# Top-k attention and a gated feed-forward layer on one core: eight units turned by TensorE in place of four, the steps as a list, the threshold kept negated

## The chip, the cores and the metric

One core of a Trainium2 chip runs the whole program. The metric is the device time of one execution in microseconds; the median of the runs is compared. A profile of one further execution shows every instruction of the five engines: TensorE (PE, its weight loads PEld), VectorE (DVE), ScalarE (ACT), GpSimd (POOL) and SyncE (SP), which here only issues transfers.

## What is computed

```
q, k, v: 8 batches x 8 heads x 576 rows x 64, float32
scores = q k^T / 8                                (576 x 576 per head)
kth    = the 32nd largest score of each row
attn   = softmax of the scores that are >= kth, the others masked away
x      = (attn v), heads side by side             (4608 tokens x 512)
h      = x w_in                                   (512 x 2048)
out    = (h * cos h) w_out                        (2048 x 512)
```

The weights come as 64-bit floats and are decoded to 32 bits on the chip.

## The kernel before

**Units and slots.** The 4608 tokens are cut into 36 blocks of 128. A block has four units, one for each pair of heads, so there are 144 units; a unit's scores are 128 rows x 2 heads x 576. The main loop has one slot for each unit. In slot i VectorE searches unit i for its 32 largest scores a row; ScalarE masks and exponentiates unit i-1 and copies the scores of unit i+1 out of PSUM (`take_scores`, L250); unit i-2 is turned, so that keys lie on partitions; TensorE makes the scores of units i+1 or i+1 and i+2, once in four slots the value matmuls of a whole block (`values`, L465 and after), and in between the feed-forward work of earlier blocks.

**The search.** Scores are folded: `rest` holds the larger of columns k and k+288 (L267), `low` the smaller (GpSimd: a sum, L283, less `rest`, L292; in slots 8 to 10, BUSY, VectorE itself, L275). Four rounds of eight largest on `rest` and two on `low` (L359, L364) leave two sorted lists. `merge_first` and `merge_second` (L347, L352) make the threshold from them. `bounds` (L372) writes the negated maximum and threshold, `distances` (L379) their difference nd. ScalarE scales nd (L386), masks with a Prelu whose bias is the negated threshold (L388) and takes exponentials with their sums (L396). `sums` and `reciprocal` (L404, L409) make 1/sum, named rden, at the end of the search in the next slot.

**Turning a unit.** There are two ways. `turn` (L430 and after), for units 0 to 3: eight 128x128 transposes on TensorE into two PSUM banks (L438), one more for the rest of the keys (L441) and two matmuls that spread rden (L445); ScalarE copies each bank into `ring` (L439, L446). `send`, for all others: GpSimd splits the numbers into 16-bit halves (L419, L421), SP writes them to DRAM (L450) and reads them back through a transposing transfer into `ring` (L456).

**Feed-forward.** `ff1` (L562) multiplies a block by w_in, 32 matmuls to a PSUM bank; ScalarE empties it twice (`take_first`, L576 and L578), GpSimd reduces (L598, L607), ScalarE takes the sine (L617, with a table load, and another before the next exponentials), GpSimd gates (L624), `ff2` (L637) multiplies by w_out, ScalarE scales (L647) and sends the result. The PSUM tag "mm" has two banks in turn: the transposes' `tt`, the banks of `ff1` and of `ff2` all come from it.

**Weights.** 32 chunks are loaded (L120) into staging tiles, 16 of w_in and 16 of w_out; ScalarE decodes each in two operations (`decode_first`, L133 and L136), VectorE shifts (`decode_second`, L151, two chunks in one instruction where they are neighbours) and GpSimd adds (`decode_third`, L160). This goes on until slot 11.

**What sets the order.** Every engine works through its own instructions in program order and waits by semaphores. The program order of a slot is written in `slot` (L762); which feed-forward pieces go where comes from `plan` (L755), from counters in `ff` and from conditions such as `can_first` (L654). `drain` (L832) ends the program.

Of the kernel before, what the change touches and what calls it, by code (L numbers as in the profile page):

```python
# [17 lines left out]
P = 128  # L18
# [12 lines left out]
def kernel(  # L31
# [63 lines left out]
    BUSY = range(8, 11)  # L95
    ff = {"live": 0, "tick": 0, "now": 0, "end": False, "kind": 0, "half": 0, "open": 0, "late": False}

    wq = {"next": 0, "loaded": deque(), "second": deque(), "third": deque(), "done": 0, "ready": 0}

    def staged(spare=0):  # L100
        return sum(c[2] == spare for k in ("loaded", "second", "third") for c in wq[k])

    def load_weights(n, queue):
        for _ in range(n):
            i = wq["next"]
            if i >= len(chunks):
                return
            src, dst = chunks[i]
            if not DECODE:
                queue.dma_start(out=dst[0][:, dst[1]], in_=src)  # L110
                wq["next"] = wq["done"] = i + 1
                continue
            spare = i < 2 * NC + 10 and i % 2 == 1 and staged(1) < XB
            if spare:
                st = ffw.tile([P, CW, 2], I32, tag="x", name="st", bufs=XB)
            elif staged() + ff["live"] >= CHUNKS:
                return
            else:
                st = ffw.tile([P, CW, 2], I32, tag="g", name="st", bufs=CHUNKS)
            queue.dma_start(out=st.rearrange("p w i -> p (w i)"), in_=src)  # L120
            wq["loaded"].append((st, dst, int(spare)))
            wq["next"] = i + 1

# [3 lines left out]
    def decode_first(n):  # L127


        for _ in range(min(n, len(wq["loaded"]))):  # L130
            st, w, spare = wq["loaded"].popleft()
            lo, hi = st[:, :, 0], st[:, :, 1]
            nc.scalar.activation(  # L133
                out=w[0][:, w[1]], in_=hi.bitcast(F32), func=AF.Prelu, scale=2.0**-111, alpha=2.0**32
            )
            nc.scalar.mul(out=lo, in_=lo.bitcast(U32), mul=2.0**-29)  # L136
            wq["second"].append((st, w, spare))

    def decode_second(n):

        left = min(n, len(wq["second"]))
        while left:
            st, (w, c), spare = wq["second"].popleft()
            wq["third"].append((st, (w, c), spare))
            m = 1
            if left > 1 and wq["second"][0][1][0] is w:
                wq["third"].append(wq["second"].popleft())
                m = 2
            left -= m
            wi = w[:, c : c + m].bitcast(I32)  # L150
            nc.vector.tensor_scalar(  # L151
                out=wi, in0=wi, scalar1=3, scalar2=None, op0=ALU.logical_shift_left
            )

    def decode_third():

        while wq["third"]:
            st, w, _ = wq["third"].pop()
            wi = w[0][:, w[1]].bitcast(I32)
            nc.gpsimd.tensor_tensor(out=wi, in0=wi, in1=st[:, :, 0], op=ALU.add)  # L160
            wq["done"] += 1

# [69 lines left out]
    def scores(u):  # L235
        sc = u["sc"] = ps.tile([P, 2, 512], F32, tag="sc", name="sc", bufs=2)
        for to, k0, k1 in ((sc, 0, SB), (sc_ends[u["n"] % 2], SB, S)):
            for b, q0, rows, r0 in u["parts"]:
                for j in range(2):
                    d = slice(j * D, (j + 1) * D)  # L240
                    st = pairs[b, u["hp"]]
                    nc.tensor.matmul(  # L242
                        to[r0 : r0 + rows, rim_bank(r0, j) if k0 else place(u["hp"], j), 0 : k1 - k0],
                        st["q"][d, q0 : q0 + rows],
                        st["k"][d, k0:k1],
                        start=True,
                        stop=True,
                    )
# [61 lines left out]
    def topk_first(u, w):  # L310

        u["top"] = tops[u["n"] % len(tops)]
        if w:
            merge_first(w)
        if u["n"] not in BUSY:
            fold_sum(u)
        fold_high(u)
        if w:
            merge_second(w)
        if u["n"] in BUSY:  # L320
            fold_now(u)
        topk_round(u, 0, [lambda: bounds(w), lambda: distances(w)] if w else ())

    def topk_round(u, rnd, between=(), ahead=None):
        top, rest, lasts = u["top"], u["rest"], TOPK // 8 - 1
        end = TOPK - 1 - 8 * rnd
        at = top[:, :, end : end - 8 if rnd < lasts else None : -1, 0]
        search(
            at, rest[:, :, HS:S] if rnd == 0 else rest[:, :, 0:HS], rest[:, :, 0:HS], rnd < lasts,
            between if rnd < lasts else (),  # L330
        )
        if rnd < lasts:
            return
        del u["rest"]
        low = u.pop("low")
        for k in range(TOPK // 16):
            more = k < TOPK // 16 - 1
            if ahead and not more:
                ahead()
            search(top[:, :, 1 + 8 * k : 9 + 8 * k, 1], low, low, more, () if more else between)  # L340

# [7 lines left out]
    def merge_second(u):  # L351
        nc.vector.tensor_reduce(  # L352
            out=u["top"][:, :, TOPK - 1, 1], in_=u.pop("lesser"), axis=mybir.AxisListType.X,
            op=ALU.max,
        )

    def search(to, src, rest, more, between=()):
        for j in range(2):
            nc.vector.max(to[:, j], src[:, j])  # L359
            if between:  # L360
                between[j]()
        if more:
            for j in range(2):
                nc.vector.match_replace(rest[:, j], to[:, j], src[:, j], NEG)  # L364

    def bounds(u):

        top = u.pop("top").rearrange("p j r i -> p j (r i)")
        end = 2 * TOPK
        less = u["less"] = top[:, :, end : end + 2]  # L370
        u["near"] = top[:, :, end - 1 : end + 1]
        nc.vector.tensor_reduce(  # L372
            out=less, in_=top[:, :, end - 2 : end].unsqueeze(3), axis=mybir.AxisListType.X,
            op=ALU.max, negate=True,
        )

    def distances(u):
        u["nd"] = small.tile([P, 2], F32, tag="nd", name="nd")
        nc.vector.tensor_reduce(  # L379
            out=u["nd"], in_=u.pop("near"), axis=mybir.AxisListType.X, op=ALU.add  # L380
        )

    def mask(u):

        s, less = u["s"], u.pop("less")
        nc.scalar.mul(out=u["nd"], in_=u["nd"], mul=SCALE)  # L386
        for j in range(2):
            nc.scalar.activation(  # L388
                out=s[:, j], in_=s[:, j], func=AF.Prelu, bias=less[:, j, 1:2], scale=1.0, alpha=FAR
            )  # L390

    def exponentials(u):
        s, nd = u["s"], u.pop("nd")
        den = u["den"] = dens[u["n"] % len(dens)]
# [16 lines left out]
    def both(u):  # L411
        return [lambda: sums(u), lambda: reciprocal(u)] if u else ()

    def split(u):


        s = u.pop("s").rearrange("p j k -> p (j k)").bitcast(U16)
        halves = work.tile([P, 2, 2 * S + P], U16, tag="halves", name="halves", bufs=1)
        nc.gpsimd.tensor_copy(out=halves[:, :, 0 : 2 * S], in_=s.rearrange("p (k h) -> p h k", h=2))  # L419
        rden = u.pop("rden").bitcast(U16).rearrange("p (j h) -> p h j", h=2)  # L420
        nc.gpsimd.tensor_copy(  # L421
            out=halves[:, :, 2 * S :].rearrange("p h (j d) -> p h j d", j=2),
            in_=rden.unsqueeze(3).to_broadcast([P, 2, 2, D]),
        )
        u["halves"] = halves
# [4 lines left out]
    def turn(u):  # L430

        s = u.pop("s").rearrange("p j k -> p (j k)")
        pT = u["pT"] = ring[:, u["n"] % RING]
        for half in range(2):
            tt = ps.tile([P, 512], F32, tag="mm", name="tt", bufs=2)
            for c in range(NT):
                at = (half * NT + c) * P
                nc.tensor.transpose(tt[:, c * P : (c + 1) * P], s[:, at : at + P], ident)  # L438
            nc.scalar.copy(out=pT[:, half * NT : (half + 1) * NT], in_=tt.rearrange("p (c q) -> p c q", c=NT))  # L439
        at = 2 * NT * P  # L440
        nc.tensor.transpose(room[0][:, P : 2 * P], s[:, at : at + P], ident)  # L441
        rden = u.pop("rden")
# [3 lines left out]
        nc.scalar.copy(out=pT[:, 2 * NT :], in_=rim[:, :, 3 * P :])  # L446
# [43 lines left out]
    def take_values(us):  # L490
# [4 lines left out]
        while i < n:  # L495
            at, h = us[i]["n"] % RING, (hp + i) // 2
            m = 4 if n - i == 4 and at + 4 <= RING else 2 if at + 2 <= RING else 1
            if m > 1:
# [7 lines left out]
            else:  # L506
                for k in range(i, i + 2):
# [3 lines left out]
                    )  # L511
                m = 2
            i += m
        blk["left"] -= n
        blk["tick"] = ff["tick"]


# [393 lines left out]
```

## Time and profile before

| | us |
|---|---|
| median of 3 runs | 1412.59 (1412.39 to 1415.35) |
| span of the profiled execution | 1410.6 |
| TensorE busy in it | 1354.9 |
| VectorE busy | 1344.2 |
| GpSimd busy | 1164.8 |
| ScalarE busy | 1139.4 |
| share of the 16 DMA engines, queue 1 | 60.8% |

The profile gives the span of its execution, from the first instruction to the last, and no other time of it; the median of the runs lies 2.0 us above that span. An engine's busy time counts its instructions, not its waits. In a row of the order in time, the bracket at the end is the idle time of the engine before that row, and what ended it. Matmuls overlap each other; what tells their pace is the distance from start to start.

### The profile page before, as it was taken

The numbers are of one execution on the slowest core, as the hardware profiler recorded it, in microseconds if no ns is written. First come the engines' busy times: TensorE is split into PE (matmuls) and PEld (weight loads), VectorE is DVE, ScalarE is ACT, GpSimd is POOL, SyncE is SP. The second block draws the span as 40 slices with busy tenths as digits, with TensorE's granted clock in tenths as the row PEclk, the third lists the DMA queues.
The fourth block names the chain that finished last, engine by engine and source line by source line (L and its number), as shares of the span: only waits on it lengthen the run. The fifth ranks groups of instructions, "written<-read, shape, count | busy, mean of one in ns | idle before, by whom it ended". The sixth has DMA issues, their size and how long they took to land.

```text
span 1410.6 us, 32356 instructions
## 1 busy us (share of the span) xinstructions
PE 1354.9 (96%) x11264; PEld 976.6 (69%) x11264; DVE 1344.2 (95%) x5148; ACT 1139.4 (81%) x2043; POOL 1164.8 (83%) x804
## 2 busy tenths in 40 slices
PE   4568999999999999999999999999999999999998
PEld 2445777777777777777777777777777777777775
DVE  7999999999999999999999999999999999999931
ACT  6987888888888888888888888888888888888831
POOL 5778988898888888888888888888888888888810
PEclk7688999999999999999999999999999999999999
DMA  8566876767675575677666677666776666555540
GB/s 274 198 207 180 205 184 165 206 174 192 155 185 151 165 194 158 176 169 194 174 172 160 142 188 186 171 169 161 207 164 168 158 172 172 142 157 148 150 101 15
DMA packets 427443, 240.13 MB, mean 170 GB/s; under 512 B 375952, under 2 KB 392592, under 8 KB 427280
## 3 DMA queue, kind: packets, MB, share of 16 engines
q1 hardware_dynamic: 420720, 224.22, 60.8%
q10 hardware_dynamic: 6560, 13.85, 2.8%
q8 instruction: 88, 1.44, 0.4%
q14 instruction: 75, 0.61, 0.1%
HBM read 45.09 MB, written 101.19 MB: 104 GB/s over the span
## 4 chain that ended last, share of the span: by engine, by line
PE 83%; DVE 10%; ACT 4%; DMA 2%; SPq 0%; issue 0%; ACTq 0%; DVEq 0%
PE o L637 32%; PE mm L562 32%; PE rim L484 10%; PE sc L242 7%; DVE top L359 5%; DVE rest L364 3%; PE rim L242 2%; DMA st<-in_moe_w_in_dram 2%; DVE rest L267 1%; DVE low L364 1%; ACT s L396 1%; ACT st L136 1%; ACT s L388 1%; ACT w_out L133 0%; ACT w_in L133 0%; ACT ring L439 0%
## 5 line engine op out<-in xcount | busy, mean ns | idle before, releaser
L562 PEld LDWEIGHTS mm<-xT,w_in 128*128 128x128 f32 x4608 | 538.3, 192 | 70.8 <-issue 55.7
L562 PE MATMUL mm<-xT,w_in 128*128 128x128 f32 x4608 | 540.0, 276 | 2.2 <-DVE xT L500 1.3
L637 PE MATMUL o<-w_out,g 128*128 128x512 f32 x1152 | 524.7, 599 | 0.0
L359 DVE MAX8 top<-rest 128x8 f32<-128x288 f32 x1152 | 478.7, 451 | 0.0
L364 DVE MATCH_REPLACE8 rest<-top,rest 128x288 f32<-128x288 f32 x864 | 376.4, 443 | 0.0
L637 PEld LDWEIGHTS o<-w_out,g 128*128 128x128 f32 x1152 | 207.7, 190 | 219.5 <-issue 219.2
L419 POOL COPY halves<-s 128x2304 uint16<-128x2304 uint16 x140 | 294.6, 2104 | 51.4 <-ACT s L396 48.2
L359 DVE MAX8 top<-low 128x8 f32<-128x288 f32 x576 | 241.6, 448 | 0.4 <-POOL low L292 0.3
L396 ACT ACTIVATE s<-s,nd 128x576 f32<-128x576 f32 x288 | 220.6, 770 | 0.8
L292 POOL TENSOR_TENSOR low<-low,rest 128x576 int32<-128x576 int32 x141 | 199.3, 1413 | 11.0
L388 ACT ACTIVATE s<-s,top 128x576 f32<-128x576 f32 x288 | 205.7, 762 | 0.0
L283 POOL TENSOR_TENSOR low<-s 128x576 int32<-128x576 int32 x141 | 198.9, 1411 | 5.7 <-ACT s L259 5.7
L386 ACT ACTIVATE nd<-nd 128x2 f32<-128x2 f32 x144 | 29.5, 205 | 177.1 <-DVE nd L379 177.0
L607 POOL TENSOR_TENSOR x<-g,x 128x1024 f32<-128x1024 f32 x68 | 160.8, 2364 | 5.7
L624 POOL TENSOR_TENSOR g<-g,x 128x1024 f32<-128x1024 f32 x68 | 160.8, 2365 | 0.0
L242 PE MATMUL sc<-k,q 64*64 64x448 f32 (+1 forms) x1120 | 145.3, 564 | 15.7 <-DMA k<-in_k_dram 8.6
L484 PE MATMUL rim<-ring,v 128*64 128x128 f32 (+1 forms) x2560 | 138.1, 267 | 0.0
L484 PEld LDWEIGHTS rim<-ring,v 128*64 128x64 f32 x2560 | 129.0, 139 | 6.4 <-issue 5.9
L253 ACT COPY s<-sc 128x896 f32<-128x896 f32 (+1 forms) x144 | 128.5, 892 | 2.7 <-PE sc L242 2.7
L364 DVE MATCH_REPLACE8 low<-top,low 128x288 f32<-128x288 f32 x288 | 125.4, 443 | 0.0
L257 ACT COPY s<-rim 64x256 f32<-64x256 f32 (+1 forms) x280 | 103.0, 368 | 26.6 <-PE rim L484 24.9
L598 POOL TENSOR_SCALAR x<-x 128x1024 f32<-128x1024 int32 x68 | 71.2, 1047 | 63.5 <-ACT x L578 63.5
(56 smaller groups left out, 1272.3 us busy)
## 6 DMA issues: line engine op xcount, KB each, us to landing
rows<-halves SPq DMA_DIRECT2D x140, 640.0 KB, 3.5
out_dram<-ob ACTq DMA_DIRECT2D x36, 256.0 KB, 2.1
q<-in_q_dram SPq DMA_DIRECT2D x31, 288.0 KB, 4.3
st<-in_moe_w_in_dram SPq DMA_DIRECT2D x16, 512.0 KB, 6.9
v<-in_v_dram SPq DMA_DIRECT2D x32, 256.0 KB, 4.3
k<-in_k_dram SPq DMA_DIRECT2D x31, 144.0 KB, 4.2
k<-in_k_dram SPq DMA_DIRECT2D x32, 128.0 KB, 4.5
st<-in_moe_w_out_dram SPq DMA_DIRECT2D x8, 512.0 KB, 5.1
```

Source lines behind the costliest of these rows:

```text
L242: nc.tensor.matmul(to[r0 : r0 + rows, rim_bank(r0, j) if k0 else place(u["hp"], j), 0 : k1 - k0], st["q"][d, q0 : q0 + rows], st["k"][d, k ...
L283: nc.gpsimd.tensor_tensor(out=u["low"].bitcast(I32), in0=s[:, :, 0:HS], in1=s[:, :, HS:S], op=ALU.add)
L292: nc.gpsimd.tensor_tensor(out=low, in0=low, in1=u["rest"][:, :, HS:S].bitcast(I32), op=ALU.subtract)
L359: nc.vector.max(to[:, j], src[:, j])
L364: nc.vector.match_replace(rest[:, j], to[:, j], src[:, j], NEG)
L388: nc.scalar.activation(out=s[:, j], in_=s[:, j], func=AF.Prelu, bias=less[:, j, 1:2], scale=1.0, alpha=FAR)
L396: nc.scalar.activation(out=s[:, j], in_=s[:, j], func=AF.Exp, bias=nd[:, j : j + 1], scale=SCALE, accum_out=den[:, j, 0:1],)
L419: nc.gpsimd.tensor_copy(out=halves[:, :, 0 : 2 * S], in_=s.rearrange("p (k h) -> p h k", h=2))
L484: nc.tensor.matmul(to[d, r], lhsT, rhs, start=(bank, j) not in begun, stop=c == NT - 1 and u in us[-2:] and r0 + rows == P,)
L562: nc.tensor.matmul(mm[:, at : at + w], w_in[f // FC][:, c, (f % FC) * P : (f % FC + 1) * P], blk["xT"][:, c], start=c == 0, stop=c == NC - 1,)
L607: nc.gpsimd.tensor_tensor(out=x, in0=g, in1=x, op=ALU.subtract)
L637: nc.tensor.matmul(o, g[:, at : at + P], w_out[f], start=f == 0, stop=f == NF - 1)
```

## The change

1. Units 4 to 7 are turned by TensorE too, in slots 6 to 9; the other way starts with unit 8.
2. The program order is a list of steps, executed one by one; `slot`, `plan`, the conditions and `drain` are gone. For example `T1.4` makes the first four transposes of unit 4 and `T1e.4` copies their bank out; `F1.0.2` is the third piece of `ff1` of block 0 and `B1.0.1` empties its second bank; `M`, `E` and `K` are mask, exponentials and copy of scores, `D1`, `D2` and `D3` the three decodes, `L` a weight load, `P0` the fold with the merge of the unit before, `R` and `Q` the rounds, `C` hands sums and reciprocal to the next round, `sp`, `wr`, `tr` the way over DRAM, `V` and `X` the value matmuls and their scaling.
3. `merge_second` writes the negated threshold, which is the mask's bias at once; `bounds` is gone. `distances` adds the maximum and the negated threshold and now follows the first search instruction of the slot; nd is scaled by -1/8 just ahead of the exponentials, where it was scaled by 1/8 ahead of the mask.
4. The shift of the decode is one instruction for each chunk. All weight loads are issued by SP; the last eight were issued by ScalarE.
5. At the very end sums and reciprocal of the last unit come when they are first asked for.

```diff
     def merge_second(u):
         nc.vector.tensor_reduce(
             out=u["top"][:, :, TOPK - 1, 1], in_=u.pop("lesser"), axis=mybir.AxisListType.X,
-            op=ALU.max,
-        )
+            op=ALU.max, negate=True,
+        )
+        u["less"] = u["top"].rearrange("p j r i -> p j (r i)")[:, :, 2 * TOPK - 1 : 2 * TOPK]
...
-    def bounds(u):
-
-        top = u.pop("top").rearrange("p j r i -> p j (r i)")
-        end = 2 * TOPK
-        less = u["less"] = top[:, :, end : end + 2]
-        u["near"] = top[:, :, end - 1 : end + 1]
-        nc.vector.tensor_reduce(
-            out=less, in_=top[:, :, end - 2 : end].unsqueeze(3), axis=mybir.AxisListType.X,
-            op=ALU.max, negate=True,
-        )
...
     def mask(u):
-
-        s, less = u["s"], u.pop("less")
-        nc.scalar.mul(out=u["nd"], in_=u["nd"], mul=SCALE)
+        s, less = u["s"], u["less"]
         for j in range(2):
             nc.scalar.activation(
-                out=s[:, j], in_=s[:, j], func=AF.Prelu, bias=less[:, j, 1:2], scale=1.0, alpha=FAR
+                out=s[:, j], in_=s[:, j], func=AF.Prelu, bias=less[:, j], scale=1.0, alpha=FAR
             )
     def exponentials(u):
         s, nd = u["s"], u.pop("nd")
+        nc.scalar.mul(out=nd, in_=nd, mul=-SCALE)
...
+    def turn(u, half):
+        u["pT"] = ring[:, u["n"] % RING]
+        s = rows_of(u)
+        tt = u["tt", half] = ps.tile([P, 512], F32, tag="mm", name="tt", bufs=2)
+        for c in range(NT):
+            at = (half * NT + c) * P
+            nc.tensor.transpose(tt[:, c * P : (c + 1) * P], s[:, at : at + P], ident)
+
+    def take_turn(u, half):
+        nc.scalar.copy(
+            out=u["pT"][:, half * NT : (half + 1) * NT],
+            in_=u.pop(("tt", half)).rearrange("p (c q) -> p c q", c=NT),
+        )
...
+fs.7 P0.7 R0.7 R0m.7 fl.7 R1.7 R2.7 D2.24 D2.25 D3.25 D3.24 F1.0.2 F1.0.3 M.6 E.6 B1.0.1 K.8
+R3.7 Q0.7 C.6 Q1.7 D1.26 D1.27 A0.0.0 A.0.0 L.28.g L.29.g T1.6 T1e.6 T2.6 T2e.6 T3.6 T3e.6 P0.8
+P0b.8 R0.8 R0m.8 R1.8 R2.8 D2.26 D2.27 D3.27 D3.26 F1.0.4 F1.0.5 Sa.9 Sb.9 Sa.10 Sb.10 M.7
+B1.0.2 E.7 K.9 R3.8 Q0.8 C.7 Q1.8 D1.28 D1.29 T1.7 T1e.7 T2.7 T2e.7 T3.7 T3e.7 P0.9 P0b.9 R0.9
...
+    for step, *of in order:
+        steps[step](*of)
```

## The prediction

> **What bounds the kernel now.** I read the page first, then busy times by stretch, then the chain of waits, and last the order in time on single engines. The page says which engine has no room:
>
> ```profile
> span 1410.6 us, 32356 instructions
> PE 1354.9 (96%) x11264; PEld 976.6 (69%) x11264; DVE 1344.2 (95%) x5148; ACT 1139.4 (81%) x2043; POOL 1164.8 (83%) x804
> ```
>
> Two engines near 100% can't both set the pace. The chain of waits decides. Its first piece of each block (128 tokens, four slots; a slot is the stretch in which VectorE searches one unit) is the 80 value matmuls:
>
> ```profile
> 335.72 4.08 PE rim L484 x80
> ...
> 372.42 4.08 PE rim L484 x80
> ...
> 409.12 4.08 PE rim L484 x80
> ...
> 555.91 4.65 PE rim L484 x160
> ...
> 593.18 4.08 PE rim L484 x80
> ```
>
> Blocks are 36.70 us apart, always, except where a block crosses two batches and has 160 half-size value matmuls: that one takes 37.27 us, 0.57 more, which is what its value matmuls cost more (4.65 against 4.08). VectorE's starts of blocks vary (36.57 to 36.82). So TensorE paces, and VectorE follows with 0.1 us or so to spare. From 111.5 us to the end at 1406.9 TensorE is idle twice only: 0.65 us before 129.37 and 0.29 us before 1342.35. Whatever happens after 111.5 us on another engine is hidden unless it makes TensorE wait anew; whatever moves that start moves the end by the same amount.
>
> The start is another matter. By stretch (us, then busy us of PE, PEld, DVE, ACT, POOL with counts, TensorE clock, DMA share, GB/s):
>
> ```profile
> 50.00:75.00 25.00, 18.74 (x162) 15.13 (x162) 23.46 (x86) 21.51 (x45) 18.59 (x15) 0.67 0.52 184
> 75.00:100.00 25.00, 16.83 (x132) 14.11 (x128) 25.00 (x92) 20.01 (x41) 20.76 (x16) 0.80 0.70 196
> 100.00:125.00 25.00, 15.19 (x151) 10.82 (x152) 24.58 (x93) 20.00 (x34) 16.44 (x13) 0.80 0.61 174
> 300.00:400.00 100.00, 100.00 (x819) 72.50 (x816) 99.96 (x390) 83.55 (x150) 88.01 (x60) 1.00 0.68 176
> ```
>
> Up to about 111 us TensorE has room and VectorE has none: slots 6 to 10 begin at 69.73, 79.67, 89.40, 99.62 and 109.84 (the fold of L267), with no idle between. The four units whose transposition changes (4 to 7) fall into slots 6 to 9.
>
> **Part by part.** *Steps as a list.* On each engine the order of instructions is that of before, but for: the transposes (below); the pairwise shifts of the weight decode, now single; the scaling of nd, now behind the mask; distances, now one search earlier; the last eight weight loads, issued by SP instead of ScalarE's queue; and the last unit's sum and reciprocal, now behind one x subtraction. A pair of shifts takes 0.59 us to the next start (15.52 to 16.11), a single 0.33 (53.30 to 53.63): +0.07 for each of 13 pairs. Eight of them lie before slot 6, where VectorE waits 1.54 us at 68.08 anyway; five later ones make 0.35 us. The eight loads cost ScalarE's queue 0.3 to 0.45 us each beside its running work; on SP they stand ahead of unit 8's write, which goes out at 117.44, 10 us after the last load's issue at 106.28. Both are nothing. At the end the reciprocal moves from 1347.85 to about 1351.3 (behind the 2.08 us subtraction of 1348.85), so the last write moves from 1351.22 by up to 1.5 us; its transposition is issued by 1357.04 and wanted by TensorE at 1362.60: nothing, or 0 to 1 us if that cover fails.
>
> *Threshold negated, bounds gone.* 143 reductions of L372, 0.06 us each to the next start (508.34 to 508.40), leave VectorE: 8 us of its time, but it isn't the pacer; in slots 6 to 10 the 0.3 us just pays for the shifts. The mask no longer waits for nd. ScalarE's idle before it was 2.44 us in slot 7 and 2.43 in slot 8, none in 6 and 9. In the steady part earlier masks feed nothing that TensorE waits for; they remove the 0.29 us at 1342.35 (mask waits 1.58 us less there). I take -0.3.
>
> *Four more units by TensorE.* GpSimd loses 4 x (2.10 + 0.40) us and SP four writes and four transpositions. GpSimd paces nothing here and the value matmuls at 113.44 wait for no transfer: nothing. TensorE gains 4 x 11 instructions, ScalarE 4 x 3 copies:
>
> ```profile
> 59.02 1.16 ACT L439 COPY ring<-tt 128x512 f32<-128x512 f32 x2
> 59.96 0.48 ACT L446 COPY ring<-rim 128x256 f32<-128x256 f32 x1
> 60.23 0.32 ACT L386 ACTIVATE nd<-nd 128x2 f32<-128x2 f32 x1
> ...
> 91.79 0.20 ACT L386 ACTIVATE nd<-nd 128x2 f32<-128x2 f32 x1 [2.43 <-DVE nd L379]
> ...
> 107.79 0.88 ACT L253 COPY s<-sc 128x896 f32<-128x896 f32 x1
> ```
>
> So 1.21 us a unit (59.02 to 60.23), 4.84 in all, which by itself just eats the 4.87 us of idle that the earlier mask frees: ScalarE's copy of unit 10's scores would again end at 109.3, just in time for the fold of 109.84. But a new ring of waits comes with it. Transposes and the feed-forward matmuls share tag "mm", two PSUM banks in turn. The first F1 matmul of a slot now takes the bank of T1 of that slot, so it waits for T1e; T1e stands on ScalarE behind the slot before's weight decodes (D1); and ScalarE's B1, then the exponentials and the next scores (K) wait for the 32 matmuls. Before, the F1 of a slot ran up to 7 us ahead of it (slot 8's ended at 82.3). Now, in order, with rows of before: D1 1.18 a chunk, T1e 0.47, all T 1.21, mask 1.34, B1 1.04, nd 0.10, E 1.52 (2.83 with the table), K 1.05 (1.55 in two pieces), sine with table 2.35, and 32 F1 matmuls 3.73 at full clock:
> - Slot 6: decodes end 71.49, T1e 71.96, F1 75.7; mask done 74.04, so 1.7 us idle; B1 76.7, E 78.4, K 79.4. The fold of 79.67 just makes it.
> - Slot 7: D1 81.8, T1e 82.2, F1 86.0, E (ahead of B1) 85.9, B1 87.0, K 88.6; fold 89.40 in time.
> - Slot 8: D1 90.9, T1e 91.4, F1 95.1, mask 93.5, B1 96.1, E 97.8, K 99.3; fold 99.62 just in time.
> - Slot 9: D1 101.7, T1e 102.1, F1 105.9, sine 105.2, mask 106.6, B1 107.6, E 110.5, K 112.05. The fold of 109.84 waits: +2.2 us.
>
> That is with TensorE at full clock throughout. The clock was not full where it idled:
>
> ```profile
> 83.50:86.90 3.40, 0.00 (x0) 0.00 (x0) 3.40 (x11) 3.39 (x9) 2.64 (x3) 1.00 0.47 193
> 86.90:90.30 3.40, 0.70 (x8) 0.31 (x8) 3.40 (x14) 2.43 (x5) 3.32 (x4) 0.50 1.11 234
> 90.30:93.70 3.40, 2.65 (x18) 1.42 (x19) 3.40 (x14) 1.89 (x4) 3.40 (x2) 0.50 1.01 257
> 93.70:97.10 3.40, 3.40 (x18) 3.40 (x17) 3.40 (x13) 3.39 (x9) 1.54 (x3) 0.50 0.53 210
> ```
>
> After 3.4 us with little work the granted clock is 0.5 until a stretch of 3.4 us is nearly full; the F1 run at 93.18 took 5.71 us, 2.0 more. (The Trainium skill, "TensorE: Matmul & The Clock Gate", Part 1, has the same rule, half clock after an idle window of about 3.4 us, with windows that run free of the program; the rows agree, and the free phase is why two executions can differ here. By its number alone, 3.4 us at half speed, an F1 run would lose an estimated 1.7 us.) In slots 8 and 9 TensorE now has only some transposes between about 87 and 91 us and between 98 and 102, so I take the half clock there: +2.0 in slot 8, and +1.3 in slot 9, where the sine hides 0.7. In slots 6 and 7 the gaps before F1 are about 2 us, so I take none; bounds are 0 and +2.0 each. The value matmuls of slot 10 started 0.8 us before the clock came up; after a longer idle it may be up to 3.4, so 0 to +1.4, I take 0.5.
>
> Sum: 2.2 + 3.3 + 0.5 - 0.3 = +5.7 us on the span of 1410.6 us, so 1416.3. That page shows no more than the span of its execution; the median of the runs, 1412.59, lies 2.0 above it, and I carry the 2.0: 1418.3. Ends: no half clock, +1.9; everything at half, 2.2 + 7.3 + 1.4 - 0.3 = +10.6.
>
> **Rivals.** *The ring at full clock only.* If the transposes keep the windows busy enough, +1.9: 1414.5. For it: the stretch 97.10 to 100.50, only half busy, kept the full clock. Against: slot 8 would have under 1 us of work in 3.4.
>
> *Not slower: the copies just fill the freed idle.* If F1 does not wait for T1e (a free bank), ScalarE gains 4.84 and loses 4.87 us, slot 10 starts at 109.84 as before, and with the 0.3 at the end it is 1412.3. It is decided where the first F1 matmul of slot 8 starts: before the first ring copy of that slot, or after it. For it: GpSimd's relief and the freed waits are real. Against: the rotation of the two banks, counted through from the warm-up.
>
> *Faster: VectorE is the pacer after all.* It is busy 99.96 of 100 us. Then 143 x 0.06 us come off in full, 1404.0 without a loss at the start. Against: the blocks of exactly 36.70 us, and 37.27 where only TensorE has more to do.
>
> *The ring reaches further.* If slot 9's lateness spoils the steady part too (GpSimd's first gate late, the output matmuls at about 118 waiting), 1424 or more. GpSimd loses ten us of work, which speaks against it.
>
> **How the numbers follow.** The runs of before differ by up to 2.96 us, so about 0.2%, 2.8 us, is what can be told from no change. Forecast 0.70; full clock only 0.11, mostly within 0.2%; copies hidden 0.10; VectorE pacer 0.04; further 0.05. Slower by over 0.2% is 0.70 + 0.03 + 0.05 = 0.78, within 0.18, faster 0.04. The range goes from the low end's 1414.5, rounded down, to the +10.6: 1414.0 to 1423.2; what lies below is the hidden and the faster case, what lies above a part of the last.
>
> **What would show it.** Right: slots 6 to 10 start at about 69.7, 79.7, 89.4, 101 and 115 us; the first F1 matmul of slots 6 to 9 right after the first ring copy of its slot, with idle before it named after ScalarE; blocks still 36.70 us apart from slot 10 on; the nd row's 177 us of idle gone. Wrong: slot 10 at 110 us or earlier, or blocks that are shorter than 36.70.

## The result, and the profile after

| | before | after |
|---|---|---|
| median (range) | 1412.59 us (1412.39 to 1415.35) | 1421.63 us (1420.21 to 1422.66) |
| span of the profiled execution | 1410.6 us | 1418.0 us |
| TensorE, VectorE busy | 1354.9, 1344.2 us | 1364.7, 1336.9 us |

The ratio after to before is 1.0059, 95% interval 1.0048 to 1.0070: 9.0 us slower. The two spans differ by 7.4 us; the rest, 1.6 us, is the distance from span to median, 3.6 us after and 2.0 us before.

Lines of the code are those of the changed kernel from here on: fold L241, the threshold L338, mask L369, nd scaled L375, exponentials L378, sum L386, copies of a unit's scores (K) L227 and L231, decode (D1) L115 and L119, the scores L216, the second fold (`low`) L249, transposes L421 and L432, spread of rden L438, ring copies L424 and L441, F1 L532, B1 L548 and L550, F2 L581, value matmuls L479, sine L570.

The head of the page of the changed kernel:

```profile
span 1418.0 us, 32333 instructions
PE 1364.7 (96%) x11316; PEld 985.1 (69%) x11316; DVE 1336.9 (94%) x5017; ACT 1153.7 (81%) x2055; POOL 1154.7 (81%) x796
```

VectorE lost 7.3 us of work and GpSimd 10.1, and the time still rose. The chain of waits after the change (start, length, what):

```profile
159.62 4.08 PE rim L479 x80
196.32 4.08 PE rim L479 x80
233.02 4.65 PE rim L479 x160
270.29 4.08 PE rim L479 x80
...
1400.58 13.75 PE o L581 x32
```

and two pieces of the chain before:

```profile
151.62 4.08 PE rim L484 x80
...
1393.17 13.75 PE o L637 x32
```

Blocks are 36.70 us apart as before, and 37.27 after a block with 160 value matmuls. The block that began at 151.62 before begins 8.00 us later; the last row, at 1393.17 before, comes 7.41 later. So all of the loss was made ahead of 159.62, and some 0.6 us came back at the end. The order in time on VectorE, the start of slots 6 to 10:

```profile
69.04 0.75 DVE L241 TENSOR_TENSOR rest<-sc,s 128x576 f32<-128x576 f32 x1
78.97 0.75 DVE L241 TENSOR_TENSOR rest<-sc,s 128x576 f32<-128x576 f32 x1
89.71 0.76 DVE L241 TENSOR_TENSOR rest<-sc,s 128x576 f32<-128x576 f32 x1 [1.06 <-ACT s L231]
101.23 0.16 DVE L386 TENSOR_REDUCE den<-dens 128x2 f32<-128x4 f32 x1 [1.88 <-ACT s L378]
102.67 0.76 DVE L241 TENSOR_TENSOR rest<-sc,s 128x576 f32<-128x576 f32 x1 [0.65 <-ACT s L231]
115.40 0.16 DVE L386 TENSOR_REDUCE den<-dens 128x2 f32<-128x4 f32 x1 [3.09 <-ACT s L378]
116.84 0.76 DVE L241 TENSOR_TENSOR rest<-sc,s 128x576 f32<-128x576 f32 x1 [0.65 <-ACT s L231]
```

The same start of slots 9 and 10 before:

```profile
99.62 0.75 DVE L267 TENSOR_TENSOR rest<-sc,s 128x576 f32<-128x576 f32 x1
...
109.84 0.75 DVE L267 TENSOR_TENSOR rest<-sc,s 128x576 f32<-128x576 f32 x1
```

VectorE, without idle here before, waits for ScalarE: 1.06 us ahead of slot 8, 2.53 (1.88 + 0.65) ahead of slot 9, 3.74 ahead of slot 10, 7.33 in all. Against before the slots stand at -0.69, -0.70, +0.31, +3.05 and +7.00 us. TensorE in the same stretch:

```profile
69.61 5.09 PE L532 MATMUL mm<-xT,w_in 128*128 128x128 f32 x32
...
81.58 5.46 PE L532 MATMUL mm<-xT,w_in 128*128 128x128 f32 x32 [2.04 <-ACT ring L424]
...
92.72 5.46 PE L532 MATMUL mm<-xT,w_in 128*128 128x128 f32 x32 [2.29 <-ACT ring L424]
...
105.66 5.47 PE L532 MATMUL mm<-xT,w_in 128*128 128x128 f32 x32 [2.27 <-ACT ring L424]
...
121.39 4.71 PE L479 MATMUL rim<-ring,v 128*64 128x128 f32 x64
...
137.37 3.84 PE L532 MATMUL mm<-xT,w_in 128*128 128x128 f32 x32 [0.64 <-ACT x L550]
```

Before, none of the four F1 runs waited for a copy, and those of slots 7 and 8 ran ahead in one piece:

```profile
74.96 7.41 PE L562 MATMUL mm<-xT,w_in 128*128 128x128 f32 x64
```

Three of the four F1 runs now wait about 2.2 us for the slot's first ring copy (L424), and all four take 5.1 to 5.5 us, where a run at full clock takes 3.84. ScalarE has the other half of the ring (F1 waits for T1e, and B1, with the copy K behind it, waits for F1), its idle time ahead of B1:

```profile
87.08 0.60 ACT L548 ACTIVATE g<-mm 128x512 f32<-128x512 f32 x1 [1.71 <-PE mm L532]
...
98.28 0.60 ACT L548 ACTIVATE g<-mm 128x512 f32<-128x512 f32 x1 [3.52 <-PE mm L532]
...
111.16 0.60 ACT L548 ACTIVATE g<-mm 128x512 f32<-128x512 f32 x1 [1.00 <-PE mm L532]
```

In the groups of the page the idle time that was named at the scaling of nd (177.1 us, for VectorE) is gone; what is left of it stands at the mask, and B1 (25.6 us before) has new waits:

```profile
L369 ACT ACTIVATE s<-s,top 128x576 f32<-128x576 f32 x288 | 207.6, 768 | 95.5 <-DVE top L338 74.1
L548 ACT ACTIVATE g<-mm 128x512 f32<-128x512 f32 x144 | 85.3, 592 | 71.9 <-PE mm L532 70.9
```

Only 9.6 us of B1's 71.9 lie in slots 6 to 9 (3.36, 1.71, 3.52 and 1.00). The rest is spread over the steady part, where blocks stayed 36.70 us apart, so it cost nothing there.

By stretch, cut every 3.41 us where the granted clock changes (bounds and length; busy us of PE, PEld, DVE, ACT, POOL with counts; the clock; DMA share; GB/s):

```profile
79.11:82.52 3.41, 1.37 (x13) 1.13 (x13) 3.41 (x13) 3.41 (x8) 3.33 (x3) 1.00 0.81 293
82.52:85.93 3.41, 3.41 (x18) 3.41 (x18) 3.41 (x13) 2.82 (x7) 0.85 (x2) 0.50 0.37 150
85.93:89.34 3.41, 2.21 (x18) 1.73 (x17) 2.73 (x12) 2.25 (x5) 3.05 (x3) 1.00 0.45 131
89.34:92.75 3.41, 0.73 (x6) 0.37 (x6) 3.04 (x10) 3.36 (x7) 2.43 (x2) 1.00 0.06 25
92.75:96.17 3.42, 3.42 (x16) 3.42 (x17) 3.42 (x14) 2.01 (x4) 0.00 (x0) 0.50 0.02 5
...
102.99:106.41 3.42, 1.15 (x11) 0.91 (x11) 3.42 (x12) 3.38 (x8) 0.00 (x0) 1.00 0.01 4
106.41:109.82 3.41, 3.41 (x18) 3.41 (x17) 3.41 (x14) 3.40 (x4) 0.04 (x1) 0.50 0.00 0
```

A stretch in which TensorE worked 1.37, 0.73 or 1.15 us of 3.41 is followed by one at half clock, and that one holds the F1 run. After 2.21 us the clock stayed full. None of these stretches ahead of an F1 run was without work; gaps of 2.0 to 2.3 us were enough. The value matmuls of slot 10 follow a stretch with no work at all (113.24 to 116.65), and 64 of them take 4.71 us, where 3.71 before.

### The profile page after: what moved, and what is told of

Read it like the earlier page. It is cut to its first block, busy times and chain, and to the rows that moved or that the text cites. A ratio compares the mean times of both kernels' runs of the same rounds, so it can differ in the third digit from the quotient of the medians.

```text
span 1418.0 us, 32333 instructions
## 1 busy us (share of the span) xinstructions
PE 1364.7 (96%) x11316; PEld 985.1 (69%) x11316; DVE 1336.9 (94%) x5017; ACT 1153.7 (81%) x2055; POOL 1154.7 (81%) x796
## 4 chain that ended last, share of the span: by engine, by line
PE 92%; DVE 4%; ACT 3%; DMA 0%; issue 0%; POOL 0%; SPq 0%; POOLq 0%; ACTq 0%
PE mm L532 37%; PE o L581 35%; PE rim L479 10%; PE sc L216 8%; PE rim L216 2%; DVE top L350 2%; DVE rest L357 1%; ACT s L378 0%; DVE w_in L131 0%; DVE low L357 0%; DVE rest L241 0%; ACT w_out L115 0%; ACT st L119 0%; ACT s L227 0%; ACT s L231 0%; DMA st<-in_moe_w_in_dram 0%
## 5 line engine op out<-in xcount | busy, mean ns | idle before, releaser
L532 PEld LDWEIGHTS mm<-xT,w_in 128*128 128x128 f32 x4608 | 542.9, 194 | 75.6 <-issue 65.9
L532 PE MATMUL mm<-xT,w_in 128*128 128x128 f32 x4608 | 544.4, 277 | 7.2 <-ACT ring L424 6.6
L581 PE MATMUL o<-w_out,g 128*128 128x512 f32 x1152 | 524.7, 599 | 0.0
L581 PEld LDWEIGHTS o<-w_out,g 128*128 128x128 f32 x1152 | 207.7, 190 | 219.5 <-issue 214.8
L396 POOL COPY halves<-s 128x2304 uint16<-128x2304 uint16 x136 | 286.4, 2106 | 46.1 <-ACT s L378 43.0
L369 ACT ACTIVATE s<-s,top 128x576 f32<-128x576 f32 x288 | 207.6, 768 | 95.5 <-DVE top L338 74.1
L378 ACT ACTIVATE s<-s,nd 128x576 f32<-128x576 f32 x288 | 221.0, 768 | 3.3
L216 PE MATMUL sc<-k,q 64*64 64x448 f32 (+1 forms) x1120 | 145.5, 562 | 6.2 <-DVE top L350 4.6
L231 ACT COPY s<-rim 64x256 f32<-64x256 f32 (+1 forms) x280 | 102.8, 367 | 54.0 <-PE rim L479 52.4
L548 ACT ACTIVATE g<-mm 128x512 f32<-128x512 f32 x144 | 85.3, 592 | 71.9 <-PE mm L532 70.9
L479 PE MATMUL rim<-ring,v 128*64 128x128 f32 (+1 forms) x2560 | 137.6, 266 | 0.0
L479 PEld LDWEIGHTS rim<-ring,v 128*64 128x64 f32 x2560 | 128.6, 138 | 6.5 <-issue 5.7
L227 ACT COPY s<-sc 128x896 f32<-128x896 f32 (+1 forms) x144 | 127.7, 887 | 3.2 <-PE sc L216 3.2
L241 DVE TENSOR_TENSOR rest<-sc,s 128x576 f32<-128x576 f32 x144 | 107.7, 748 | 9.3 <-ACT s L233 6.5
```

The source lines that it names most:

```text
L216: nc.tensor.matmul(to[r0 : r0 + rows, rim_bank(r0, j) if k0 else place(u["hp"], j), 0 : k1 - k0], st["q"][d, q0 : q0 + rows], st["k"][d, k ...
L369: nc.scalar.activation(out=s[:, j], in_=s[:, j], func=AF.Prelu, bias=less[:, j], scale=1.0, alpha=FAR)
L378: nc.scalar.activation(out=s[:, j], in_=s[:, j], func=AF.Exp, bias=nd[:, j : j + 1], scale=SCALE, accum_out=den[:, j, 0:1],)
L479: nc.tensor.matmul(to[d, r], lhsT, rhs, start=(bank, j) not in begun, stop=c == NT - 1 and u in us[-2:] and r0 + rows == P,)
L532: nc.tensor.matmul(blk["mm"][:, at : at + w], w_in[f // FC][:, c, (f % FC) * P : (f % FC + 1) * P], blk["xT"][:, c], start=c == 0, stop=c ...
L581: nc.tensor.matmul(blk["o"], blk["g"][f // 8][:, f % 8 * P : (f % 8 + 1) * P], w_out[f], start=f == 0, stop=f == NF - 1,)
```

## The experiments

Each kernel was timed beside the kernel before on the same chip, which had medians of 1413.14 us beside e1 to e4, 1413.37 beside e5 to e7, 1412.13 beside e8 and e9 and 1413.21 beside e10; the ratios are to these. "Slots" are the starts of slots 8, 9 and 10, "F1" the lengths of the F1 runs of slots 6 to 9, "V" the first value matmul of slot 10 (before: 89.40, 99.62, 109.84; V 113.44).

| kernel | median us | ratio (95%) | slots | F1 | V |
|---|---|---|---|---|---|
| the change | 1421.63 | 1.0059 (1.0048 to 1.0070) | 89.71, 102.67, 116.84 | 5.09, 5.46, 5.46, 5.47 | 120.38 |
| e1 four turned | 1413.23 | 0.9998 (0.9990 to 1.0007) | 89.80, 100.02, 110.25 | - | 113.85 |
| e2 only turns | 1421.34 | 1.0059 (1.0046 to 1.0071) | 87.97, 101.54, 116.67 | 5.44, 3.84, 6.62, 6.53 | 120.22 |
| e3 turn late | 1412.98 | 0.9997 (0.9988 to 1.0006) | 88.26, 98.49, 109.73 | 3.81, 3.84, 5.88, 3.84 | 114.63 |
| e4 warm | 1416.27 | 1.0025 (1.0015 to 1.0034) | 88.80, 99.90, 113.00 | 5.44, 3.84, 3.84, 3.84 | 116.54 |
| e5 folds on GpSimd | 1412.98 | 1.0001 (0.9992 to 1.0009) | 88.45, 98.06, 110.10 | 3.81, 3.84, 6.04, 3.84 | 115.05 |
| e6 and decode | 1413.21 | 0.9998 (0.9990 to 1.0007) | 89.32, 98.98, 109.94 | 3.81, 3.84, 5.45, 3.84 | 114.62 |
| e7 copies first | 1415.11 | 1.0010 (1.0001 to 1.0019) | 88.53, 98.80, 111.74 | 3.84, 5.16, 5.47, 3.84 | 115.28 |
| e8 sine later | 1410.08 | 0.9984 (0.9975 to 0.9993) | 88.28, 97.89, 107.48 | 3.81, 3.84, 5.89, 3.84 | 111.02 |
| e9 and warm | 1415.43 | 1.0023 (1.0013 to 1.0033) | 88.68, 98.32, 107.92 | 5.44, 3.84, 3.84, 3.84 | 115.65 |
| e10 turned again | 1409.03 | 0.9971 (0.9959 to 0.9983) | 88.41, 98.06, 107.66 | 3.81, 3.84, 3.84, 3.84 | 110.24 |

**Which of the edits costs: e1 and e2.** e1 is the changed kernel with units 4 to 7 sent over DRAM, e2 the kernel before with nothing but the four more turned units (the first pair of lines is e1's list of steps for unit 4, the second e2's code):

```diff
-T1.4 T1e.4 T2.4 T2e.4 T3.4 T3e.4
+sp1.4 sp2.4 wr.4 tr.4
...
-(turn if i < NP + 2 else send)(x)
+(turn if i < 2 * NP + 2 else send)(x)
```

> The changed kernel with units 4 to 7 sent over DRAM again, at the place in the list where their transposes stood; all other edits stay. Theory (the turns of units 4 to 7 cost everything): slot 10 begins again at about 109.8 us, blocks 36.70 us apart, time 1412.3, 0 to 0.5 us below before. Rival (a part of the loss comes from the single shifts, nd behind the mask, or the loads on SP): it stays above before by that part, 1414 to 1418.

> The kernel before with one edit: units 0 to 7 are turned by TensorE. Theory: the same ring, bank of T1, then F1, then B1, so slot 10 begins near 117 us and the time is 1421 to 1422 as with the whole change; the mask's wait for nd is hidden behind ScalarE's copies. Rival (the earlier mask matters to the ring): 2 to 4 us above the changed kernel, 1424.

e1 is the time of before (0.1 us from it), e2 that of the change (0.3 us from it, and the same ratio). So the turned units are the whole loss, and the list of steps, the negated threshold, the single shifts and the moved loads together are worth nothing that can be measured. The 0.6 us that the tail gains in the trace drown in it.

**Whether it is the work or its place: e3.** The same instructions, with the steps T of each of the four units behind Q1 of their slot and ahead of the next weight decodes:

```diff
-Q1.5 D1.21 D1.22 D1.23 L.24.g L.25.g T1.4 T1e.4 T2.4 T2e.4 T3.4 T3e.4 fs.6
+Q1.5 D1.21 D1.22 D1.23 L.24.g L.25.g fs.6
...
+Q1.6 T1.4 T1e.4 T2.4 T2e.4 T3.4 T3e.4 D1.24 D1.25
```

> The changed kernel with the same transposes, but each of units 4 to 7 turned at the end of its slot, behind the last search and ahead of the next decodes, so that no F1 waits for decodes and no transpose for rden. Nothing is taken away. Theory (the place in the order costs, not the work): F1 runs ahead again, slot 10 begins at 109.5 to 111 us, time 1412 to 1414. Rival (TensorE's and ScalarE's added work costs by itself): 1418 to 1422.

The time is that of before. The F1 runs of slots 6 to 9 come at 67.91, 76.48, 86.37 and 97.39, 0.8 to 2.2 us ahead of their slots, and none waits for a bank. The transposes wait now, and the time shows no loss by it. TensorE in e3:

```profile
97.39 3.84 PE L532 MATMUL mm<-xT,w_in 128*128 128x128 f32 x32
101.06 0.60 PE L421 MATMUL tt<-ident,s 128*128 128x128 f32 x4
105.29 1.11 PE L421 MATMUL tt<-ident,s 128*128 128x128 f32 x4 [3.62 <-ACT x L550]
109.75 0.47 PE L432 MATMUL rim<-ident,s 128*128 128x128 f32 x1 [3.35 <-ACT s L231]
```

So 44 instructions of TensorE and 12 copies of ScalarE cost nothing that the medians show, and their position is the loss. The traces say the same: the block that begins at 151.62 before begins at 152.43 in e3 and at 152.87 in e1, which has none of these instructions.

**Which part of the position: e7.** Only the first two steps and their copies go ahead of the decodes of the slot before; T3 and T3e stay:

```diff
-Q1.5 D1.21 D1.22 D1.23 L.24.g L.25.g T1.4 T1e.4 T2.4 T2e.4 T3.4 T3e.4 fs.6
+Q1.5 T1.4 T1e.4 T2.4 T2e.4 D1.21 D1.22 D1.23 L.24.g L.25.g T3.4 T3e.4 fs.6
```

> The change, with the first two transposes' steps and their copies (T1 T1e T2 T2e of units 4 to 7) moved ahead of the decodes of the slot before; the rest of the keys and rden (T3, T3e) stay. If the F1 matmuls are late because T1e stands behind the decodes, F1 of slots 7 to 9 starts about 2 us earlier (no wait after the ring copy), the waits of ScalarE before B1 go, and the time is 1414 to 1417 us. Rival (F1 is late because the two banks rotate through any transposes of the slot, or T3 with its wait for rden is the term): F1 as in the change, 1420 to 1422 us.

TensorE in e7:

```profile
79.50 5.16 PE L532 MATMUL mm<-xT,w_in 128*128 128x128 f32 x32
...
88.84 5.47 PE L532 MATMUL mm<-xT,w_in 128*128 128x128 f32 x32
...
99.44 3.84 PE L532 MATMUL mm<-xT,w_in 128*128 128x128 f32 x32
```

The rows have no bracket: the wait behind L424 is gone, and F1 starts 0.57, 0.31 and 0.64 us after the slot, where the change has 2.61, 3.01 and 2.99. Some 6.5 of the 9 us come back (1421.63 to 1415.11), with two F1 runs still at half clock. T1e behind the decodes is thereby shown as the cause of that wait. T3's wait for rden isn't: it is still there in e7 (1.26 and 0.79 us ahead of the spread of rden in slots 7 and 8). What makes up the remaining 1.7 us above the kernel before is not taken apart.

**How much of it is the clock: e4.** The changed kernel, with twelve idle transposes of the identity (a step W makes four) behind T3 of units 5, 6 and 7, in the gap before F1:

```diff
-T3.5 T3e.5
+T3.5 W.0 W.0 W.0 T3e.5
```

> The changed kernel with twelve idle transposes of the identity (three W steps) after T3 of units 5, 6 and 7, in the time in which TensorE waits for T1e. They add work and compute nothing. Theory of the clock term: the granted clock stays full, the F1 runs of slots 7, 8 and 9 take 3.7 us in place of 5.5, and the time falls by 3 to 5 us, to 1417 to 1419. Rival (only the wait counts, not the clock): no change or slower, 1421 to 1423.

TensorE in e4:

```profile
79.84 1.53 PE L887 MATMUL rim<-ident 128*128 128x128 f32 x12
81.98 3.84 PE L532 MATMUL mm<-xT,w_in 128*128 128x128 f32 x32 [0.61 <-ACT ring L424]
...
102.94 3.84 PE L532 MATMUL mm<-xT,w_in 128*128 128x128 f32 x32 [0.86 <-ACT ring L424]
```

and by stretch:

```profile
78.80:82.20 3.40, 2.39 (x20) 1.85 (x20) 3.13 (x12) 3.40 (x8) 3.32 (x3) 1.00 0.90 322
85.60:89.00 3.40, 1.80 (x15) 1.17 (x14) 3.40 (x14) 3.29 (x8) 3.33 (x3) 1.00 0.29 58
```

Work that computes nothing and does not shorten the wait for L424 gains 5.4 us by the medians (4.8 by the ratios): the F1 runs of slots 7 to 9 and the value matmuls are back at full clock (3 x 1.62 + 1.0 = 5.9 us of TensorE). The rest of the loss, 3.1 us by the medians (3.5 by the ratio), is put down to the ring at full clock. The gains of e7 and e4 (6.5 and 5.4 us) are more than the 9.0 together, so they overlap: the wait that the order makes is also the gap ahead of the half clock.

**What sets the start of slot 10: e5, e6, e8.** In e3 VectorE waits 0.18 and 0.65 us for ScalarE ahead of slot 10, which starts at 109.73, as ScalarE's copy K of unit 10 ends. The last step of unit 7's turn waits for the same copy (109.75, above), and from there TensorE reaches the first value matmul at 114.63 without a wait. e5 takes the folds of slots 8 to 10 from VectorE, e6 also the low half of five chunks from ScalarE; e8 has the folds of slots 8 and 9 on GpSimd, as e5, leaves slot 10's on VectorE and moves the sine of block 0 out of slot 9:

```diff
-    BUSY = [8, 9, 10]
+    BUSY = []
...
-P0.8 P0b.8 R0.8 R0m.8 R1.8
+fs.8 P0.8 R0.8 R0m.8 fl.8 R1.8
...
-    LOW_BY_POOL = []
+    LOW_BY_POOL = [21, 22, 23, 24, 25]
...
-D2.24 D2.25 D3.25 D3.24
+D2.24 D2.25 D0.24 D0.25 D3.25 D3.24
...
-F1.0.6 F1.0.7 N.0.0 M.8 B1.0.3 E.8 K.10
+F1.0.6 F1.0.7 M.8 B1.0.3 E.8 K.10
...
-T3.7 T3e.7 G.0.0 A0.0.1 A.0.1
+T3.7 T3e.7 N.0.0 A0.0.1 A.0.1 G.0.0
```

> The change, with the four units turned at the end of their slot as in e3, and with the folds of slots 8 to 10 taken from VectorE (0.67 us in each of these slots) and given to GpSimd as in all other slots. Ring theory: in e3 VectorE and ScalarE reach the fold of slot 10 together (109.73 and about 109.7), so the gain of VectorE is held up by ScalarE's copy of unit 10's scores: slot 10 at 109 to 109.7, 1411 to 1413 us. Rival (VectorE alone sets the start): slot 10 at 107.7, 1411.0 or less. Second rival (GpSimd's decode, fold, reductions and gate don't fit into slot 9, about 11 us of work): slot 10 after 110.5, 1414 or more.

> e5, with the low half of five weight chunks (21 to 25) scaled by GpSimd in place of ScalarE (5 x 0.58 = 2.9 us off ScalarE ahead of slot 9). If both engines together set the start of slot 10, as the ring theory has it, it comes at 107 to 107.5, the value matmuls of block 1 at about 110.5 (e3: 114.63), 1409.5 to 1410.5 us: under both kernels. Rival (the start is set by something else, such as the weight loads, 0.70 of the 16 DMA engines in 75 to 100 us, or GpSimd): no better than e5, 1412 to 1414 us.

> e3, with the sine of block 0 (a table load of 1.28 us and 1.15 us, and another table load of 1.28 us ahead of the exponentials behind it) moved from the middle of slot 9 to behind the copies of unit 7, where ScalarE later waits 3.8 us for the value matmuls, with the gate behind GpSimd's first reductions, and with the folds of slots 8 and 9 on GpSimd. In e5 and e6 ScalarE had no idle of over 0.04 us from 92.7 to 109.7, whatever was taken off ahead of it. If that stretch of ScalarE sets the start of slot 10, ScalarE's copy of unit 10 now ends near 106.1, VectorE sets the start at 107.3 to 107.7 and the value matmuls of block 1 start at 111.5 to 113 (e3: 114.63): 1409.5 to 1411.5 us. Rival (the gate comes too late for the output matmuls, or the delayed ScalarE makes TensorE wait later, at the 0.66 us of 130.18): 1412 us or more.

e5 and e6 gain nothing, and e6 is a miss: with 2.9 us of ScalarE's work gone, slot 10 begins at 109.94. What was freed lay ahead of ScalarE's waits. In both, ScalarE has no wait from B1 of slot 8 (92.70 and 92.57) to K of unit 10 (ending at 110.1 and 109.9), so only work inside that stretch counts. The two ends of that stretch of ScalarE in e6, with the last wait that it has ahead of it:

```profile
92.57 0.60 ACT L548 ACTIVATE g<-mm 128x512 f32<-128x512 f32 x1 [0.87 <-PE mm L532]
...
109.17 0.74 ACT L231 COPY s<-rim 64x256 f32<-64x256 f32 x2
```

e8 takes the sine and two table loads out of it (1.28 + 1.15 + 1.28 us):

```profile
105.25 0.75 ACT L231 COPY s<-rim 64x256 f32<-64x256 f32 x2
...
111.02 0.70 PE L479 MATMUL rim<-ring,v_tail 64*64 64x128 f32 x16
```

K of unit 10 ends at 106.0, 3.7 us earlier than in e3, slot 10 starts at 107.48 without a wait, and the first value matmul at 111.02, 2.4 us before the kernel before. The sine then lies in slot 10, where ScalarE in e3 waits 3.78 us for the value matmuls. e8 is under both kernels (1410.08 us, interval below 1).

**The clock once more: e9 and e10.** e9 puts idle transposes into the waits of e8. e10 fills them with the transposes of the same tiles, once more into the bank that they have just written. For unit 7 the first pair of lines is e9's against e8, the line behind it e10's (TW is the step that repeats four transposes the given number of times):

```diff
-T1.7 T1e.7 T2.7 T2e.7 T3.7 T3e.7
+T1.7 W.0 W.0 W.0 T1e.7 T2.7 W.0 W.0 T2e.7 T3.7 T3e.7
...
+T1.7 TW.7.0.2 T1e.7 T2.7 TW.7.1.4 T2e.7 T3.7 T3e.7
...
+    def turn_again(u, half, times):
+        s, tt = u["s"].rearrange("p j k -> p (j k)"), u["tt", half]
+        for _ in range(times):
+            for c in range(NT):
+                at = (half * NT + c) * P
+                nc.tensor.transpose(tt[:, c * P : (c + 1) * P], s[:, at : at + P], ident)
```

> e8, with idle transposes (as in e4; 8, 8 and 20 of them) in TensorE's waits between the transposes of units 5, 6 and 7. In e3 the scores of slot 10 and F1 of slot 8 ran at half clock (16 matmuls of 64x448 in 3.49 us against 1.91; 5.88 against 3.84 us). If the clock theory holds here, F1 of slots 6 to 9 takes 3.84 us each, the scores of slot 10 about 2 us less, and the value matmuls start 1.5 to 2 us ahead of e8's: 1408 to 1410 us. Rival (the copy of ScalarE ahead of them sets their start, or the idle transposes come into the way): as e8 or up to 1 us more.

> e8, with TensorE's waits filled by transposing the same four tiles again into the same bank: 24 more transposes behind the first four of unit 5 (e8 waits 3.15 us there), 8 and 16 behind the first and second four of unit 7 (waits of 1.17 and 2.54 us). Unlike the idle transposes of e9, which wrote into the bank that ScalarE's copy of the scores reads and so waited for it themselves (4.14 us at 107.87), these have the bank already. Clock theory: F1 of slot 8 takes 3.84 us in place of 5.89, the scores of slot 10 run at full clock (1.91 us for 16 of 64x448 in place of 3.52), and the value matmuls start 1.5 to 2 us ahead of e8's 111.02: 1408 to 1409 us. Rival (the waits behind them, for ScalarE's copy and VectorE's fold at 107.48, set the start, and the clock doesn't matter): as e8, 1410 us, or up to 1 us more.

e9 missed by 5 us or more. TensorE in e9:

```profile
107.87 2.82 PE L887 MATMUL rim<-ident 128*128 128x128 f32 x12 [4.14 <-ACT s L231]
110.49 1.06 PE L421 MATMUL tt<-ident,s 128*128 128x128 f32 x4
```

The idle transposes write into the bank of the last keys, which K (L231) reads, so they waited for K themselves, and the real transposes behind them came at 110.49 in place of 102.86. The filler was a wait of its own. (In e4 the filler writes into the same bank, but behind T3, which has waited for it already.) In e10 it has its bank already (the code there is seven lines longer from L428 on, and L428 makes the repeated transposes):

```profile
102.04 1.91 PE L428 MATMUL tt<-ident,s 128*128 128x128 f32 x16
...
109.22 0.98 PE L216 MATMUL sc<-k,q 64*64 64x448 f32 x8 [2.65 <-DVE low L249]
...
110.24 0.62 PE L486 MATMUL rim<-ring,v_tail 64*64 64x128 f32 x16
```

F1 of slot 8 takes 3.84 us and the scores run at full clock (0.98 us for eight, 1.77 in e8), as expected, but then they wait 2.65 us for VectorE's second fold. The first value matmul is 0.78 us ahead of e8's 111.02, not 1.5 to 2: VectorE sets the start there, as the rival has it. The intervals of e8 and e10 overlap; both are under the kernel before, e10 by 4.2 us, and that e10 beats e8 is not shown.

## Why the prediction was right, and where it was short

The time, 1421.63 us, lies in the stated range and 3.3 us above the forecast of 1418.3. The range held because its upper end has all four F1 runs at half clock, which is what happened (5.09 to 5.47 us).

- *The side and the mechanism: right.* The F1 matmuls wait for T1e behind the decodes (2.04, 2.29, 2.27 us, named after L424), B1 waits for F1, and the fold waits for K. e2, e3 and e7 show it by making the loss, removing it, and removing most of it with the first copies alone. Blocks of 36.70 us and TensorE as the pacer held too; VectorE's 7.3 us came off and moved nothing, so the rival of VectorE as pacer falls. With e1 at the time of before, so does every cost in the other edits. "The copies just fill the freed idle" is decided where the prediction said: F1 of slot 8 starts at 92.72, behind the first ring copy, which starts at 92.08. "The ring at full clock only" falls with e4, where filler against the half clock alone gains 4.8 to 5.4 us. "The ring reaches further" isn't seen: the lag is 6.94 us at the first value matmul (120.38 against 113.44), 8.00 at 159.62, and the 1.0 between them is the half clock of the value matmuls.
- *The clock term was mis-sized; it is the step that failed.* The prediction took half clock in slots 8 and 9 (2.0 + 1.3), 0.5 in the value matmuls, and for slots 6 and 7: "In slots 6 and 7 the gaps before F1 are about 2 us, so I take none". Slot 7's run took 5.46 us after a stretch with 1.37 us of work in 3.41: one gap of 2.04 us inside a stretch did what a long idle does. The term was 3.8 us, and e4 measured 4.8 to 5.4. (The Trainium skill, "TensorE: Matmul & The Clock Gate", Part 1, gives half clock after an idle window; here 1.37 us of work in the window did not save it. The estimated 1.7 us per run from its 3.4 us agrees with 5.46 - 3.84 = 1.62.) Slot 6's run was at half clock as well (5.09), but e1, where unit 4 isn't turned, has 5.44 there: there it follows a wait of 1.88 us for block 0's xT (in the change T3, just ahead of F1, waits 2.34 us for it), so it comes without the turned unit too.
- *The ring at full clock: 2.2 forecast, 3.1 to 3.5 measured (e4).* K of unit 10 ends at 112.97 in e4, forecast 112.05. ScalarE runs from 95.50 to there without a wait; B1 of slot 8 was 0.4 us late (the forecast has it behind F1 of 95.1), and nd's scaling directly ahead of the exponentials made E with nd 1.77 us (96.56 to 98.33), not 1.62. At full clock the prediction let the fold wait at slot 10 alone; in e4 VectorE waits 0.65 us ahead of slots 7 and 9 already. With its clock term it let slots 9 and 10 start late; in the change the waits began at slot 8.
- *Slots.* Forecast 69.7, 79.7, 89.4, 101 and 115; measured 69.04, 78.97, 89.71, 102.67 and 116.84. The first two are early because the value matmuls of block 0 ended 2.9 us earlier in this execution (64.77 against 67.63; 64 of them took 4.60 us, before 6.07), which the prediction had no term for. How much of the loss on the span that hid is not shown; 0.7 us, the lead of slots 6 and 7, is the most by our estimate.
- *The tail:* -0.3 forecast, -0.6 in the trace.
- *Span to median:* the 2.0 us carried over was 3.6 us here, since the profiled execution of the change was the fastest of its runs (1420.21). Of the 3.3 us between forecast and median 1.7 lie in the span and 1.6 here.

## What to carry to other kernels

Work moved to another engine is priced by its place in that engine's order and by the buffers it takes in turn: here the same transposes and copies cost 9 us ahead of the banks' next user and nothing behind it. Where an engine is to be relieved, find the stretch in which it never waits; work taken off ahead of a wait (e6) buys nothing, and work moved out of the stretch into a later wait (e8) buys most of it: 3.7 us of ScalarE brought the first value matmul 3.6 us forward, from e3 to e8, and the time 2 to 3 us. In a stage where TensorE has little to do, count its work per stretch (of 3.4 us in these traces), not its longest gap; filler can hold the clock, if it writes where nobody else has business.

## What the runs showed of the hardware that was not expected

- In the change the clock fell to half after stretches of 3.41 us with 1.37, 1.15 and 0.73 us of matmul work at full clock, and stayed full after 2.21; in e4 it stayed full after 1.80 of 3.40. An F1 run of 3.84 us then takes 5.1 to 5.5 us, and in e2 6.53 and 6.62. Which slot is hit changes from run to run (slot 7 in the change, not in e2).
- Twelve transposes of the identity in each of three waits made the changed kernel 5.4 us faster (e4), while 36 of them, written into a bank that another engine was about to read, made it over 5 us slower (e8 to e9).
- GpSimd got rid of 10.1 us and SP of four writes and four reads back, and VectorE of 7.3 us; by e1 and e3 none of it is worth anything that can be measured here.
